# Sums of operands by accumulating DMAs, signs of weights on VectorE, and a seventh product in three parts, in a two-layer Strassen network

## The chip, the core and the metric

One core of one Trainium2 chip. The metric is device time in microseconds (us) of one execution. The engines are TensorE (PE; its weight loads are shown as PEld), VectorE (DVE), ScalarE (ACT), GpSimd (POOL) and SyncE (SP). Each works through its own list of instructions in order; semaphores make one wait for another. DMAs are issued by SP, ACT or POOL and run on 16 DMA engines.

## The reference

Attention (batch 2, 12 heads, 448 positions, head size 64) with a tanh cap on the scores, and behind it two feed-forward layers on 896 tokens of 768 numbers, with results in float32 (the weights arrive as float64):

```python
scores = cap * np.tanh(scale * np.matmul(q, k.transpose(0, 1, 3, 2)) / cap)
attn = np.exp(scores - scores.max()); attn = attn / (attn.sum() + 1e-9)
x = merge_heads(np.matmul(attn, v))                  # 896 x 768
h = x @ w_in;  g = np.maximum(h, 0) + alpha * np.minimum(h, 0);  x = g @ w_out    # layer 1, 768 -> 2048 -> 768
h = x @ w_in2; r = np.maximum(h, 0); g = r * r;                  x = g @ w_out2   # layer 2
```

## The kernel before

The tokens stand as two halves b = 0, 1 of 448 columns. A matrix product in full float32 accuracy is made of three matmuls in the faster type fp32r: each operand is split into a high part h (a copy to fp32r, on ACT) and a low part l (operand minus h, on DVE), and hh, lh and hl are added in PSUM. A "plain" product is one float32 matmul without splits. `multiply` (L193) makes either.

After the attention there are four stages. **Up, layer 1**: for each of 16 rows f of 128 features, one weight tile of 128 x 768, and for both halves a group of 6 x 3 matmuls into one PSUM bank; then L270 and L272 on ACT and L273 on DVE give the leaky ReLU g[b, f]. For f below 3 the weights (and b = 0) are made beside the attention. **Down, layer 1**: the 2048 x 768 product is done as a 2 x 2 block product in seven products P7, P1, P2, P6, P5, P4, P3 (Winograd's form), each of 4 weight tiles (`factor`) and 8 token tiles (`tokens`), for 3 PSUM banks. Their operands are sums of quarters: S3 = A11 - A21, S2 = A22 - S3, S1 = A11 + S2, S4 = A12 - S2 of the weights, T3, T2, T1, T4 of the tokens, all made in place by `sum` (L249) on DVE. P1 alone is plain (`PLAIN`, L33; L195). The results are combined on DVE (L329) and split for layer 2 (L320 on ACT, L321 on DVE). **Up and down, layer 2** are the same, with a squared ReLU (L270, and L276 in place on ACT) and the output DMA at the end (L317).

The weights come as float64 (two int32 words each), and `load` makes float32 of one tile of 128 x 768: a DMA on SP (L223) to one of two raw buffers; ACT scales the high words into w (L239); DVE shifts the low words (L240); ACT writes a half-precision product of the high word into the top half of the low word, which leaves the sign there (L233); DVE joins w and the low words (L237). There are 64 loads: 3 beside the attention, by `read` (L173), which takes the sign with an AND and an OR on DVE (L181, L183), and 61 by `load`. Of the 32 loads of each layer 16 are up tiles and 16 down quarters; the quarters come one after the other as soon as the buffers (two raw, 16 w) allow.

The order of every instruction of the four stages on PE, ACT, DVE, POOL and SP is written out by a planner in the kernel (`Plan`): it goes through the operations in a simulated time with a cost for each and a lag to its successors, and lets each engine take the ready operation with the lowest number. Operations marked `port` (on DVE and POOL) don't overlap in it.

Of the kernel before, what the change touches and what calls it, by code (L numbers as in the profile page):

```python
# [17 lines left out]
P = 128  # L18
# [34 lines left out]
class Plan:  # L53
# [4 lines left out]
    def tag(self, name, tiles):  # L58
        self.free[name], self.queue[name] = list(tiles), []

    def op(self, engine, cost, emit, reads=(), writes=(), port=False, lag=0.06):
        op = Op(len(self.ops), engine, cost, emit, port, lag)
        self.ops.append(op)
        before = []
        for buf in reads:
            before.append(buf.writer)
        for buf in writes:
            before += [buf.writer, *buf.readers]
        for other in set(before):
# [12 lines left out]
        for buf in op.bufs:  # L82
            buf.left += 1

    def order(self):
# [8 lines left out]
        while events:  # L94
# [50 lines left out]
class Net:  # L145
# [54 lines left out]
    def activate(self, g, t, ps, f):  # L200
        nc = self.nc
        nc.scalar.activation(g, ps, AF.Relu)
        nc.scalar.activation(t, ps, AF.Relu, scale=-1.0)
        nc.vector.scalar_tensor_tensor(g, t, self.slope_t[:, f:f + 1], g, op0=ALU.mult, op1=ALU.add)

    def up_now(self, f):

# [11 lines left out]
    def load(self, src):  # L219

        nc, plan, n = self.nc, self.plan, self.NC * P
        raw, w = Buf("raw"), Buf("w")
# [8 lines left out]
        def sign():
            halves = raw.tile.bitcast(F16).rearrange("p n (f t) -> p n f t", t=4)
            nc.scalar.mul(halves[:, :, :, 1], parts()[1].bitcast(F32), 2.0 ** -60)  # L233
# [11 lines left out]
    def sum(self, out, a, b, op, n, engine="DVE", inplace=True):  # L245
        nc, plan = self.nc, self.plan
        e = {"DVE": nc.vector, "POOL": nc.gpsimd}[engine]
        cost = self.dve(n) if engine == "DVE" else 0.15 + 0.0024 * n
        plan.op(engine, cost, lambda: getattr(e, op)(out.tile, a.tile, b.tile), [a, b], [out], port=True)  # L249

    def split(self, w, tags, n, engine="DVE"):
# [3 lines left out]
        e = {"DVE": nc.vector, "POOL": nc.gpsimd}[engine]  # L255
        plan.op(engine, self.dve(n) if engine == "DVE" else 0.15 + 0.0024 * n,
                lambda: e.tensor_sub(l.tile, w.tile, h.tile.bitcast(F32)), [w, h], [l], port=True)  # L257
        return h, l

    def products(self, ps, w, x, c, first, last):  # L260
        self.plan.op("PE", 3 * 0.2044 if len(w) == 2 else 0.752, lambda: self.multiply(ps.tile, [b.tile for b in w], [b.tile for b in x], c, first, last),
                     [*w, *x], [ps])

    def up(self, w, f, b, first):

        nc, S, plan, half = self.nc, self.S, self.plan, self.NF // 2
        ps, g, t = Buf("ps"), Buf("g"), Buf("t")
        for c in range(self.NC):
            self.products(ps, w, self.x[b, c], c, c == 0, c == self.NC - 1)
        plan.op("ACT", self.act(S), lambda: nc.scalar.activation(g.tile, ps.tile, AF.Relu), [ps], [g])  # L270
        if first:
            plan.op("ACT", self.act(S), lambda: nc.scalar.activation(t.tile, ps.tile, AF.Relu, scale=-1.0), [ps], [t])  # L272
            plan.op("DVE", self.dve(S), lambda: nc.vector.scalar_tensor_tensor(  # L273
                g.tile, t.tile, self.slope_t[:, f:f + 1], g.tile, op0=ALU.mult, op1=ALU.add), [t, g], [g], port=True)
        else:
            plan.op("ACT", self.act(S), lambda: nc.scalar.square(g.tile, g.tile), [g], [g])  # L276
        self.g[b, f] = g
        if b == 1 and f >= half:
            self.sum(self.g[1, f - half], g, self.g[1, f - half], "tensor_sub", S)

    def quarter(self, name, i):
        a = {"A11": 0, "S3": 1, "A12": 2, "A22": 3}[name]
        w = self.a[name, i] = self.load(self.wdown[:, a * PARTS + i])
        if name == "S3":
            self.sum(w, self.a["A11", i], w, "tensor_sub", self.NC * P)

    def factor(self, name, i, plain):

        a, n = self.a, self.NC * P
        if name == "S2":  # L290
            a[name, i] = a.pop(("S3", i))
            self.sum(a[name, i], a["A22", i], a[name, i], "tensor_sub", n)
        elif name == "S1":
            a[name, i] = a.pop(("A11", i))
            self.sum(a[name, i], a["S2", i], a[name, i], "tensor_add", n)
        elif name == "S4":
            a[name, i] = a.pop(("A12", i))
            self.sum(a[name, i], a[name, i], a["S2", i], "tensor_sub", n)
        return (a[name, i],) if plain else self.split(a[name, i], ("wh", "wl"), n)

    def tokens(self, name, k, plain):

        g, half, S = self.g, self.NF // 2, self.S
        if name == "T2":
            self.sum(g[1, k], g[0, k], g[1, k], "tensor_add", S)
        elif name == "T1":
            self.sum(g[0, k], g[1, half + k], g[1, k], "tensor_sub", S)
# [15 lines left out]
    def down(self, final):  # L323
# [4 lines left out]
        def add(t, ps, x):  # L328
            plan.op("DVE", self.dve(S), lambda: nc.vector.tensor_add(t.tile, ps.tile, x.tile), [ps, x], [t])  # L329

        def keep(t, ps):
            plan.op("ACT", self.act(S), lambda: nc.scalar.copy(t.tile, ps.tile), [ps], [t])
# [1 line left out]
        for name, a, b in (("P7", "S3", "T3"), ("P1", "A11", "B11"), ("P2", "A12", "B21"), ("P6", "S2", "T2"),  # L334
# [8 lines left out]
            for j in range(J):  # L343
# [3 lines left out]
                elif name == "P1":  # L347
                    keep(u[j], ps)
                elif name == "P6":
                    add(u[j], ps, u[j])  # L350
                    self.sum(v[j], u[j], v[j], "tensor_add", S)
                else:
                    row, col, x = {"P2": (0, 0, u), "P5": (1, 1, v), "P4": (1, 0, v), "P3": (0, 1, u)}[name]
                    if name == "P5":
                        add(u[j], ps, u[j])
                    t = ps if not final else Buf("g") if name in ("P2", "P5") else x[j]
                    add(t, ps, x[j])
                    self.put(t, row * J + j, col, final)

    def layers(self):  # L360
# [12 lines left out]
        for first, src, self.wdown in ((True, self.w1, self.w2), (False, self.w3, self.w4)):  # L373
            self.a = {}
            for f in range(self.NF):
                early = first and f < AHEAD
                w = ahead[f] if early else self.split(self.load(src[:, f]), ("wh", "wl"), self.NC * P)
# [450 lines left out]
```

## Time and profile before

| | us |
|---|---|
| median of 3 runs | 566.67 (564.88 to 567.07) |
| profiled execution, its own time | 567.58 |
| its span, first to last instruction | 565.8 |
| PE busy | 538.9 (95%) |
| PE weight loads busy | 424.9 (75%) |
| DVE busy | 405.4 (72%) |
| ACT busy | 419.6 (74%) |
| POOL busy | 2.0 (0%) |
| mean granted TensorE clock | 0.991 of full speed |

A row of a group of instructions says: line, engine, operation, output <- inputs by tile names, shapes, count | busy time in us, mean ns of one | idle time of the engine just before them and what ended it. Matmuls are pipelined: their recorded length (some 0.37 us for 448 columns) overlaps with the next, so a busy PE is not PE at its peak, and the distance from one to the next is what counts.

### The profile page before, as it was taken

To read this page: it belongs to the slowest core of one execution; us is meant where nothing else is said; L and a number is where in the kernel's file an instruction comes from. 1 tells how busy PE (TensorE), PEld (TensorE's weight loads), DVE (VectorE), ACT (ScalarE), POOL (GpSimd) and SP (SyncE) were. 2 spreads that over 40 slices of the span, in tenths; PEclk is the share of its full clock that TensorE was granted. 3 is DMA by queue.
4 is the path that set the end of the run, shared out by engine and by line. 5 is a ranking of instruction groups with operands and counts; after the bars stand their busy time and mean duration, and the time that the engine had idled before them with its cause. 6 is when DMAs were issued, how large, how long until landed. Compare 5 with 4: busy or idle time off the path is not lost.

```text
span 565.8 us, 6752 instructions
## 1 busy us (share of the span) xinstructions
PE 538.9 (95%) x2556; PEld 424.9 (75%) x2556; DVE 405.4 (72%) x574; ACT 419.6 (74%) x518; POOL 2.0 (0%) x12
## 2 busy tenths in 40 slices
PE   7889899979999997998999899999999999999996
PEld 2223345969999896758898788999999984789985
DVE  1798999465567767889999964444567579989862
ACT  6999892487889878957655479999889997354550
POOL 1000000000000000000000000000000000000000
PEclk9999999999999999999999899999999999999998
DMA  6455442053454444553000035555444553010111
GB/s 198 175 175 168 133 130 59 0 168 117 162 167 120 160 144 138 166 162 116 1 2 0 0 112 168 167 168 167 137 149 162 167 168 111 2 49 2 49 50 54
DMA packets 19576, 64.23 MB, mean 114 GB/s; under 512 B 3920, under 2 KB 10576, under 8 KB 19536
## 3 DMA queue, kind: packets, MB, share of 16 engines
q1 hardware_dynamic: 19392, 63.72, 34.8%
q8 instruction: 22, 0.36, 0.3%
q14 instruction: 18, 0.15, 0.1%
q10 hardware_dynamic: 144, 0.00, 0.0%
HBM read 60.89 MB, written 2.79 MB: 113 GB/s over the span
## 4 chain that ended last, share of the span: by engine, by line
PE 48%; ACT 28%; DVE 16%; DMA 4%; issue 2%; POOL 0%; ACTq 0%; DVEq 0%; POOLq 0%
PE ps L198 28%; ACT raw L233 14%; PE hm L198 11%; DVE w L237 3%; PE ps L195 3%; ACT wh L254 3%; PE pv L516 3%; ACT w L239 3%; DMA k<-in_kT 2%; DVE wl L257 2%; ACT g L270 2%; PE ps L466 2%; DVE raw L240 2%; DVE w L249 2%; ACT xh L254 1%
## 5 line engine op out<-in xcount | busy, mean ns | idle before, releaser
L198 PE MATMUL ps<-x,wh 128*128 128x448 f32 x576 | 166.6, 370 | 3.9 <-ACT t L272 2.7
L233 ACT ACTIVATE raw<-raw 128x768 f16<-128x768 f32 x61 | 118.5, 1943 | 22.8 <-DVE raw L240 22.8
L237 DVE SCALAR_TENSOR_TENSOR w<-w,raw 128x768 int32<-128x768 int32 x61 | 58.5, 959 | 88.1 <-ACT raw L233 88.0
L198 PEld LDWEIGHTS ps<-x,wh 128*128 128x128 f32 x576 | 108.3, 189 | 17.7 <-ACT t L272 3.6
L198 PE MATMUL ps<-x,wl 128*128 128x448 f32 x288 | 106.4, 369 | 0.4 <-DVE wl L257 0.4
L254 ACT CAST xh<-g 128x448 fp32r<-128x448 f32 x93 | 52.9, 576 | 62.9 <-PE ps L198 40.9
L198 PE MATMUL ps<-xh,wh 128*128 128x448 f32 x224 | 83.9, 374 | 6.7 <-ACT t L272 3.0
L257 DVE TENSOR_TENSOR wl<-w,wh 128x768 fp32r<-128x768 f32 x77 | 73.5, 955 | 16.4 <-ACT wh L254 15.0
L198 PE MATMUL ps<-xl,wh 128*128 128x448 f32 x224 | 82.2, 367 | 0.8 <-DVE xl L257 0.8
L198 PE MATMUL ps<-xh,wl 128*128 128x448 f32 x224 | 82.3, 367 | 0.4 <-DVE wl L257 0.4
L254 ACT CAST wh<-w 128x768 fp32r<-128x768 f32 x77 | 64.8, 842 | 6.4 <-DVE w L237 4.9
L257 DVE TENSOR_TENSOR xl<-g,xh 128x448 fp32r<-128x448 f32 x93 | 56.4, 621 | 11.5 <-ACT xh L254 10.3
L198 PEld LDWEIGHTS ps<-x,wl 128*128 128x128 f32 x288 | 54.5, 189 | 5.3 <-DVE wl L257 0.7
L239 ACT ACTIVATE w<-raw 128x768 f32<-128x768 f32 x61 | 56.1, 919 | 2.0 <-DMA raw<-in_w 2.0
L198 PE MATMUL hm<-x,wh 128*128 128x448 f32 x192 | 54.6, 366 | 0.0
L198 PEld LDWEIGHTS ps<-xh,wh 128*128 128x128 f32 x224 | 42.2, 188 | 14.9 <-ACT t L272 3.6
L198 PEld LDWEIGHTS ps<-xl,wh 128*128 128x128 f32 x224 | 42.2, 189 | 4.7 <-DVE xl L257 1.2
L198 PEld LDWEIGHTS ps<-xh,wl 128*128 128x128 f32 x224 | 42.2, 188 | 4.3 <-DVE wl L257 0.7
L481 ACT ACTIVATE E<-ps,scale_t 128x896 f32<-128x896 f32 x42 | 40.3, 1022 | 5.3 <-PE ps L466 5.3
L249 DVE TENSOR_TENSOR g<-g,g 128x448 f32<-128x448 f32 x64 | 39.0, 620 | 1.0 <-ACT g L276 0.7
L198 PEld LDWEIGHTS hm<-x,wh 128*128 128x128 f32 x192 | 36.0, 187 | 3.4
L486 ACT ACTIVATE E<-E,cap_t 128x1792 f32<-128x1792 f32 (+1 forms) x24 | 38.1, 1617 | 0.0
(96 smaller groups left out, 630.7 us busy)
## 6 DMA issues: line engine op xcount, KB each, us to landing
raw<-in_w SPq DMA_DIRECT2D x64, 768.0 KB, 4.2
out_T<-g SPq DMA_DIRECT2D x12, 224.0 KB, 2.0
k<-in_kT SPq DMA_DIRECT2D x11, 224.0 KB, 4.9
q<-in_qT SPq DMA_DIRECT2D x11, 224.0 KB, 5.1
v<-in_vT SPq DMA_DIRECT2D x6, 384.0 KB, 5.2
rb<-row SPq DMA_DIRECT2D x10, 224.0 KB, 3.7
vt<-in_vt SPq DMA_DIRECT2D x6, 64.0 KB, 5.6
r<-rows SPq DMA_DIRECT2D x20, 1.8 KB, 3.6
```

The lines of the kernel that those rows point to most:

```text
L195: self.nc.tensor.matmul(ps, w[0][:, c, :], x[0], start=first, stop=last)
L198: self.nc.tensor.matmul(ps, a[:, c, :], m, start=first and n == 0, stop=last and n == 2)
L233: nc.scalar.mul(halves[:, :, :, 1], parts()[1].bitcast(F32), 2.0 ** -60)
L237: nc.vector.scalar_tensor_tensor(bits, bits, 3, parts()[0], op0=ALU.logical_shift_left, op1=ALU.bitwise_or)
L239: plan.op("ACT", self.act(n) + 0.06, lambda: nc.scalar.mul(w.tile, parts()[1].bitcast(F32), 2.0 ** -112), [high, raw], [w])
L240: plan.op("DVE", self.dve(n, 2), lambda: nc.vector.tensor_scalar(parts()[0], parts()[0], 29, None, op0=ALU.logical_shift_right), [raw], [l ...
L249: plan.op(engine, cost, lambda: getattr(e, op)(out.tile, a.tile, b.tile), [a, b], [out], port=True)
L254: plan.op("ACT", self.act(n), lambda: nc.scalar.copy(h.tile, w.tile), [w], [h])
L257: lambda: e.tensor_sub(l.tile, w.tile, h.tile.bitcast(F32)), [w, h], [l], port=True)
L481: nc.scalar.activation(es[-1][:, n % 2], ps, AF.Tanh, scale=self.scale_t)
L486: self.nc.scalar.activation(x, x, AF.Exp, scale=self.cap_t)
L516: nc.tensor.matmul(self.pv[u][rows, g, :], self.v[u][0][:, g, c, rows], self.chunk(u, g * FULL + c)[:, e], start=c == 0, stop=False)
```

## The change

P1 becomes a product of three matmuls like the other six. In `load`, the ACT instruction for the sign goes; DVE takes the sign of the high word by an AND (with an XOR where the negated tile is wanted) and ORs it to the shifted low word. Sums S3, S2, S4 of the weights and T3, T2, T4 of the tokens are no longer made on DVE but by a DMA issued from GpSimd that adds its source to its destination. [...] S1, T1 and the sums of the results stay on DVE. In layer 2 the square moves from ACT to DVE, as -g*g or max(ps, 0)*g. The planner's costs and lags are changed. The two hooks `HALF` and `SQ` are false for every tile, so the branches that use them don't run.

```diff
-PLAIN = ("P1",)
+PLAIN = ()
+HALF = (lambda f, first: False, lambda i, a: False)
+SQ = lambda f: False
+LAND = 5.0
-    def op(self, engine, cost, emit, reads=(), writes=(), port=False, lag=0.06):
+    def op(self, engine, cost, emit, reads=(), writes=(), port=False, lag=0.15):
+                        elif op.lag > 1:
+                            end, op.lag = now + op.lag, 0.3
     def act(self, n):
-        return 0.17 + 0.00084 * n
+        return 0.05 + 0.000885 * n
     def dve(self, n, rate=1):
-        return 0.16 + 0.00103 * n if rate == 1 else 0.13 + 0.00052 * n
+        return 0.075 + 0.00103 * n if rate == 1 else 0.07 + 0.00052 * n
...
-        plan.op("DVE", self.dve(n, 2), lambda: nc.vector.tensor_scalar(parts()[0], parts()[0], 29, None, op0=ALU.logical_shift_right), [raw], [low], port=True)
-        plan.op("ACT", self.act(n) + 0.06, sign, [high, raw], [low])
+        if half:
...
+        else:
+            plan.op("DVE", self.dve(n, 2), lambda: nc.vector.tensor_scalar(parts()[1], parts()[1], -(1 << 31), None, op0=ALU.bitwise_and) if sign > 0
+                    else nc.vector.tensor_scalar(parts()[1], parts()[1], -(1 << 31), -(1 << 31), op0=ALU.bitwise_and, op1=ALU.bitwise_xor), [raw], [high], port=True)
+            plan.op("DVE", self.dve(n), lambda: nc.vector.scalar_tensor_tensor(
+                parts()[0], parts()[0], 29, parts()[1], op0=ALU.logical_shift_right, op1=ALU.bitwise_or), [raw, high], [low], port=True)
         plan.op("DVE", self.dve(n), join, [low, w, raw], [w], port=True)
...
+    def gather(self, out, a):
+        nc, plan = self.nc, self.plan
+        plan.op("POOL", 1.3, lambda: nc.gpsimd.dma_start(out.tile, a.tile, accum_op=ALU.add), [a, out], [out], lag=LAND)
...
-            plan.op("ACT", self.act(S), lambda: nc.scalar.square(g.tile, g.tile), [g], [g])
+            if minus:
+                plan.op("DVE", self.dve(S), lambda: nc.vector.scalar_tensor_tensor(
+                    g.tile, g.tile, -1.0, g.tile, op0=ALU.mult, op1=ALU.mult), [g], [g], port=True)
...
+            else:
+                plan.op("DVE", self.dve(S) + 0.06, lambda: nc.vector.scalar_tensor_tensor(
+                    g.tile, ps.tile, 0.0, g.tile, op0=ALU.max, op1=ALU.mult), [g, ps], [g])
...
-            self.sum(self.g[1, f - half], g, self.g[1, f - half], "tensor_sub", S)
+            self.gather(self.g[1, f - half], g)
...
-            self.sum(w, self.a["A11", i], w, "tensor_sub", self.NC * P)
+            self.gather(w, self.a["A11", i])
...
-            self.sum(a[name, i], a["A22", i], a[name, i], "tensor_sub", n)
+            self.gather(a[name, i], a["A22", i])
...
-            self.sum(a[name, i], a[name, i], a["S2", i], "tensor_sub", n)
+            self.gather(a[name, i], a["S2", i])
...
-            self.sum(g[1, k], g[0, k], g[1, k], "tensor_add", S)
+            self.gather(g[1, k], g[0, k])
...
-            self.sum(g[0, half + k], g[0, half + k], g[1, k], "tensor_sub", S)
+            self.gather(g[0, half + k], g[1, k])
```

The leaky ReLU takes a second tile with the negated slopes and ADD or SUBTRACT by the wanted sign; P6's and P2's additions of the results become subtractions.

## Rows read from the trace of the kernel before

**Rows 1.** Busy us (x instructions) by stage; then granted clock, DMA share, GB/s.
```profile
98.00:215.00 117.00, 113.06 (x541) 102.06 (x540) 75.08 (x107) 92.66 (x117) 0.00 (x0) 0.99 0.40 128
215.00:334.00 119.00, 112.44 (x493) 92.69 (x491) 103.12 (x157) 80.40 (x112) 0.00 (x0) 0.99 0.24 75
334.00:452.00 118.00, 117.66 (x574) 107.40 (x574) 62.66 (x87) 106.66 (x130) 0.00 (x0) 1.00 0.49 159
452.00:566.00 114.00, 106.08 (x475) 88.41 (x473) 87.93 (x133) 60.29 (x88) 0.00 (x0) 0.98 0.18 60
```

**Rows 2.** The chain that ended last: start us, length us, what.
```profile
102.28 6.76 PE hm L198 x33
...
363.71 19.63 PE ps L198 x96
```

**Rows 3.** Busy time of L195 alone in the two down stages (PE, then PEld).
```profile
215.00:334.00 119.00, 18.20 (x48) 9.11 (x48) 0.99 0.24 75
452.00:566.00 114.00, 18.31 (x48) 9.04 (x48) 0.98 0.18 60
```

**Rows 4.** The timeline's last matmul: start us, length us, what.
```profile
559.89 0.37 PE L198 MATMUL ps<-xh,wl 128*128 128x448 f32 x1
```

**Rows 5.** Waits of the weight loads from 98 us on: us, times, longest.
```profile
PEld ps L198 <- ACT t L272: 7.3, 5, 3.4
...
PEld ps L198 <- ACT wh L254: 3.1, 2, 1.8
PEld ps L198 <- ACT g L332: 2.7, 2, 1.8
PEld ps L198 <- DVE x L321: 1.8, 4, 0.4
PEld ps L198 <- DVE wl L257: 1.5, 2, 0.7
PEld ps L195 <- ACT g L332: 1.4, 2, 1.3
```

**Rows 6.** Groups of instructions, shapes kept apart.
```profile
L233 ACT ACTIVATE raw<-raw 128x768 f16<-128x768 f32 x61 | 118.5, 1943 | 22.8 <-DVE raw L240 22.8
...
L257 DVE TENSOR_TENSOR wl<-w,wh 128x768 fp32r<-128x768 f32 x77 | 73.5, 955 | 16.4 <-ACT wh L254 15.0
L254 ACT CAST wh<-w 128x768 fp32r<-128x768 f32 x77 | 64.8, 842 | 6.4 <-DVE w L237 4.9 <-PE hm L198 1.1 <-DVE w L249 0.2
L237 DVE SCALAR_TENSOR_TENSOR w<-w,raw 128x768 int32<-128x768 int32 x61 | 58.5, 959 | 88.1 <-ACT raw L233 88.0
L257 DVE TENSOR_TENSOR xl<-g,xh 128x448 fp32r<-128x448 f32 x93 | 56.4, 621 | 11.5 <-ACT xh L254 10.3
...
L254 ACT CAST xh<-g 128x448 fp32r<-128x448 f32 x93 | 52.9, 576 | 62.9 <-PE ps L198 40.9 <-PE hm L198 15.3 <-DVE g L249 5.9
...
L249 DVE TENSOR_TENSOR g<-g,g 128x448 f32<-128x448 f32 x64 | 39.0, 620 | 1.0 <-ACT g L276 0.7
...
L240 DVE TENSOR_SCALAR raw<-raw 128x768 int32<-128x768 int32 x61 | 33.9, 556 | 0.1
...
L249 DVE TENSOR_TENSOR w<-w,w 128x768 f32<-128x768 f32 x32 | 30.3, 953 | 0.1
...
L273 DVE SCALAR_TENSOR_TENSOR g<-t,slope_t,g 128x448 f32<-128x448 f32 x29 | 19.7, 680 | 7.3 <-ACT t L272 7.3
...
L183 DVE SCALAR_TENSOR_TENSOR raw<-raw 128x768 int32<-128x768 int32 x3 | 3.0, 992 | 0.1
```

**Rows 7.** DMA issues: tile, queue, count, KB each, median us to landing.
```profile
raw<-in_w SPq DMA_DIRECT2D x64, 768.0 KB, 4.2
out_T<-g SPq DMA_DIRECT2D x12, 224.0 KB, 2.0
...
vt<-in_vt SPq DMA_DIRECT2D x6, 64.0 KB, 5.6
```

**Rows 8.** DVE's timeline in the down stage of layer 1.
```profile
262.90 0.95 DVE L257 TENSOR_TENSOR wl<-w,wh 128x768 fp32r<-128x768 f32 x1
263.77 0.62 DVE L257 TENSOR_TENSOR xl<-g,xh 128x448 fp32r<-128x448 f32 x1
264.30 0.95 DVE L249 TENSOR_TENSOR w<-w,w 128x768 f32<-128x768 f32 x1
```

More of the change, by code (lines that the diff above doesn't have):

```diff
@@ L203, in activate @@
         nc.scalar.activation(t, ps, AF.Relu, scale=-1.0)
-        nc.vector.scalar_tensor_tensor(g, t, self.slope_t[:, f:f + 1], g, op0=ALU.mult, op1=ALU.add)
+        nc.vector.scalar_tensor_tensor(g, t, self.slope_t[:, f:f + 1], g, op0=ALU.mult, op1=ALU.subtract)
     def up_now(self, f):
@@ L213, in act, with load @@
     def act(self, n):
-        return 0.17 + 0.00084 * n
+        return 0.05 + 0.000885 * n
     def dve(self, n, rate=1):
-        return 0.16 + 0.00103 * n if rate == 1 else 0.13 + 0.00052 * n
-    def load(self, src):
+        return 0.075 + 0.00103 * n if rate == 1 else 0.07 + 0.00052 * n
+    def load(self, src, half, sign=1):
         nc, plan, n = self.nc, self.plan, self.NC * P
@@ L229, in parts, with underflow @@
             return self.words(raw.tile)
[L231 removed]
+        def underflow():
             halves = raw.tile.bitcast(F16).rearrange("p n (f t) -> p n f t", t=4)
[L233 removed]
+            nc.scalar.mul(halves[:, :, :, 1], parts()[1].bitcast(F32), sign * 2.0 ** -60)
         def join():
@@ L239, in load, with sum, split @@
         plan.op("ACT", self.act(n) + 0.06, lambda: nc.scalar.mul(w.tile, parts()[1].bitcast(F32), 2.0 ** -112), [high, raw], [w])
-        plan.op("DVE", self.dve(n, 2), lambda: nc.vector.tensor_scalar(parts()[0], parts()[0], 29, None, op0=ALU.logical_shift_right), [raw], [low], port=True)
-        plan.op("ACT", self.act(n) + 0.06, sign, [high, raw], [low])
+        if half:
+            plan.op("DVE", self.dve(n, 2), lambda: nc.vector.tensor_scalar(parts()[0], parts()[0], 29, None, op0=ALU.logical_shift_right), [raw], [low], port=True)
+            plan.op("ACT", 1.68, underflow, [high, raw], [low])
+        else:
[3 more added lines that the diff above has]
+                parts()[0], parts()[0], 29, parts()[1], op0=ALU.logical_shift_right, op1=ALU.bitwise_or), [raw, high], [low], port=True)
         plan.op("DVE", self.dve(n), join, [low, w, raw], [w], port=True)
         return w
-    def sum(self, out, a, b, op, n, engine="DVE", inplace=True):
+    def sum(self, out, a, b, op, n):
         nc, plan = self.nc, self.plan
[L247 to L251, printed above, removed]
+        plan.op("DVE", self.dve(n), lambda: getattr(nc.vector, op)(out.tile, a.tile, b.tile), [a, b], [out], port=True)
+    def gather(self, out, a):
+        nc, plan = self.nc, self.plan
+        plan.op("POOL", 1.3, lambda: nc.gpsimd.dma_start(out.tile, a.tile, accum_op=ALU.add), [a, out], [out], lag=LAND)
+    def split(self, w, tags, n):
         nc, plan = self.nc, self.plan
@@ L254, in split @@
         plan.op("ACT", self.act(n), lambda: nc.scalar.copy(h.tile, w.tile), [w], [h])
-        e = {"DVE": nc.vector, "POOL": nc.gpsimd}[engine]
-        plan.op(engine, self.dve(n) if engine == "DVE" else 0.15 + 0.0024 * n,
-                lambda: e.tensor_sub(l.tile, w.tile, h.tile.bitcast(F32)), [w, h], [l], port=True)
+        plan.op("DVE", self.dve(n), lambda: nc.vector.tensor_sub(l.tile, w.tile, h.tile.bitcast(F32)), [w, h], [l], port=True)
         return h, l
     def products(self, ps, w, x, c, first, last):
-        self.plan.op("PE", 3 * 0.2044 if len(w) == 2 else 0.752, lambda: self.multiply(ps.tile, [b.tile for b in w], [b.tile for b in x], c, first, last),
+        self.plan.op("PE", 3 * 0.2038 if len(w) == 2 else 0.746, lambda: self.multiply(ps.tile, [b.tile for b in w], [b.tile for b in x], c, first, last),
                      [*w, *x], [ps])
@@ L267, in up @@
         ps, g, t = Buf("ps"), Buf("g"), Buf("t")
+        minus = (b == 1) == (f >= half)
         for c in range(self.NC):
@@ L272, in up @@
             plan.op("ACT", self.act(S), lambda: nc.scalar.activation(t.tile, ps.tile, AF.Relu, scale=-1.0), [ps], [t])
+            slope = self.slope_t if minus else self.minus_t
             plan.op("DVE", self.dve(S), lambda: nc.vector.scalar_tensor_tensor(
-                g.tile, t.tile, self.slope_t[:, f:f + 1], g.tile, op0=ALU.mult, op1=ALU.add), [t, g], [g], port=True)
+                g.tile, t.tile, slope[:, f:f + 1], g.tile, op0=ALU.mult, op1=ALU.subtract if minus else ALU.add), [t, g], [g], port=True)
         else:
-            plan.op("ACT", self.act(S), lambda: nc.scalar.square(g.tile, g.tile), [g], [g])
+            if minus:
+                plan.op("DVE", self.dve(S), lambda: nc.vector.scalar_tensor_tensor(
+                    g.tile, g.tile, -1.0, g.tile, op0=ALU.mult, op1=ALU.mult), [g], [g], port=True)
+            elif SQ(f):
+                plan.op("ACT", self.act(S), lambda: nc.scalar.square(g.tile, g.tile), [g], [g])
+            else:
+                plan.op("DVE", self.dve(S) + 0.06, lambda: nc.vector.scalar_tensor_tensor(
+                    g.tile, ps.tile, 0.0, g.tile, op0=ALU.max, op1=ALU.mult), [g, ps], [g])
         self.g[b, f] = g
         if b == 1 and f >= half:
-            self.sum(self.g[1, f - half], g, self.g[1, f - half], "tensor_sub", S)
+            self.gather(self.g[1, f - half], g)
     def quarter(self, name, i):
         a = {"A11": 0, "S3": 1, "A12": 2, "A22": 3}[name]
-        w = self.a[name, i] = self.load(self.wdown[:, a * PARTS + i])
+        w = self.a[name, i] = self.load(self.wdown[:, a * PARTS + i], HALF[1](i, a), -1 if a in (0, 2) else 1)
         if name == "S3":
-            self.sum(w, self.a["A11", i], w, "tensor_sub", self.NC * P)
+            self.gather(w, self.a["A11", i])
     def factor(self, name, i, plain):
@@ L304, in tokens @@
         if name == "T2":
-            self.sum(g[1, k], g[0, k], g[1, k], "tensor_add", S)
+            self.gather(g[1, k], g[0, k])
         elif name == "T1":
-            self.sum(g[0, k], g[1, half + k], g[1, k], "tensor_sub", S)
+            self.sum(g[0, k], g[1, k], g[1, half + k], "tensor_sub", S)
         elif name == "T4":
-            self.sum(g[0, half + k], g[0, half + k], g[1, k], "tensor_sub", S)
+            self.gather(g[0, half + k], g[1, k])
         x = g[{"B11": (0, k), "T3": (1, k), "B21": (0, half + k), "T2": (1, k), "T1": (0, k), "T4": (0, half + k), "B22": (1, half + k)}[name]]
@@ L326, in down, with add @@
         u, v = ([Buf("g") for _ in range(J)] for _ in range(2))
-        def add(t, ps, x):
-            plan.op("DVE", self.dve(S), lambda: nc.vector.tensor_add(t.tile, ps.tile, x.tile), [ps, x], [t])
+        def add(t, ps, x, op="tensor_add"):
+            plan.op("DVE", self.dve(S), lambda: getattr(nc.vector, op)(t.tile, x.tile, ps.tile), [ps, x], [t])
         def keep(t, ps):
@@ L356, in down @@
                     t = ps if not final else Buf("g") if name in ("P2", "P5") else x[j]
-                    add(t, ps, x[j])
+                    add(t, ps, x[j], "tensor_sub" if name == "P2" else "tensor_add")
                     self.put(t, row * J + j, col, final)
@@ L376, in layers @@
                 early = first and f < AHEAD
-                w = ahead[f] if early else self.split(self.load(src[:, f]), ("wh", "wl"), self.NC * P)
+                w = ahead[f] if early else self.split(self.load(src[:, f], HALF[0](f, first)), ("wh", "wl"), self.NC * P)
                 for b in both:
@@ L453, in constants @@
         nc.sync.dma_start(self.slope_t, self.alpha)
-        nc.gpsimd.tensor_scalar_mul(self.slope_t, self.slope_t, -1.0)
+        self.minus_t = self.const.tile([P, self.NF], F32, name="minus_t")
+        nc.gpsimd.tensor_scalar_mul(self.minus_t, self.slope_t, -1.0)
     def product(self, u, n):
```

4 lines of the change are left out of this document (2 added, 2 removed).

## The prediction

> **What bounds the kernel now.** I read the busy time by stage first, then the groups of instructions, then what TensorE waited for. The four stages after the attention are: up projection of layer 1, its down projection, and the same of layer 2. In [rows 1] the reader is to see that TensorE (PE) is busy nearly all of each stage (113.06 of 117, 112.44 of 119, 117.66 of 118, 106.08 of 114 us), and that the second engine changes: ScalarE (ACT) is at 92.66 and 106.66 us in the two up stages, VectorE (DVE) at 103.12 and 87.93 us in the two down stages.
>
> So the floor is TensorE's. In a stretch with no wait, 96 matmuls of 448 columns take 19.63 us, 0.2045 us each; the unbroken row of second-half products starts at 102.28 [rows 2]. From there the kernel has 29 groups of 18 matmuls in layer 1, 32 in layer 2 and 2 x 6 split products of 72: 1962 matmuls, 401.2 us. The plain P1 adds 18.20 and 18.31 us [rows 3]. Without a wait PE would end at 102.3 + 437.7 = 540.0. Its last matmul ends at 559.89 + 0.37 = 560.3 [rows 4]: **20.3 us are lost**. What the weight loads waited for says where: 7.3 on L272, 3.1 on L254, 2.7 and 1.4 on L332, together 14.5 us on ACT; DVE has the smaller rows (1.8 on L321, 1.5 on L257) [rows 5]. ACT is late because each weight load keeps it for L233, 1943 ns, 118.5 us over 61 loads; L237 of DVE has 88.0 us of idle time in front of it for the same instruction [rows 6].
>
> **The change part by part.**
>
> *P1 in three products.* 48 plain matmuls (36.5 us, [rows 3]) become 144 of 0.2045 = 29.4 us: **PE -7.1 us**, on the path. It adds splits of 8 weight tiles and 16 token tiles: on ACT 8 x 0.842 + 16 x 0.576 = 15.9 us, on DVE 8 x 0.955 + 16 x 0.621 = 17.6 us [rows 6]. These lie beside PE. What is lost is a breathing space: in P1 neither engine had splits to make.
>
> *Signs on VectorE.* L233 goes 61 times: **ACT -118.5 us**. DVE keeps one one-source instruction of the form of L240 (the AND in place of the shift, 556 ns for either) and gets a scalar_tensor_tensor of strided words, which the early path already has: L183, 992 ns [rows 6]. **DVE +60.5 us.** The XOR rides in the AND, at nothing. A load's chain also loses a hop between engines: AND, OR and join run one behind the other on DVE, beside the one ACT scaling.
>
> *Sums by accumulating DMA.* Of 102 sums on L249, 48 of 448 columns (T3, T2, T4) and 24 of 768 (S3, S2, S4) leave DVE: 48 x 0.620 + 24 x 0.953 = **-52.6 us** [rows 6]. No row shows an accumulating DMA or GpSimd issuing one. From below: the 224 KB output copy lands in 2.0 us; from above: the 768 KB load takes 4.2 and the slowest form 5.6 us [rows 7]. I take 5, near the upper end, as it must read two operands. What hides it: P7's last T3 operand (k = 7) is made from the last up group, and is first used after 7/8 of P7's 72 x 0.2045 = 14.7 us, so 12.9 us after P7's start; the others have one to three whole products of lead. GpSimd's queue has nothing else in it here (POOL 0.00 in all four stages, [rows 1]), but it is in order: a gather that waits for its operand holds those behind it. Their DMAs share engines that are 0.18 to 0.49 busy, with SP's loads. If the cover were gone, each microsecond over 12.9 would cost one per layer. I cost it at 0, with 0 to 6 us for the range.
>
> The row of L240 (556 ns, where two-source instructions of the same 768 columns take some 955) shows the one-source operation running at nearly twice the rate. The Trainium skill (SBUF — State Buffer, Who interferes with whom) says of just such VectorE modes that they and GpSimd exclude one another for a whole instruction, and that GpSimd then cannot write the descriptors of its DMAs; no run here shows it yet. By that rule a gather starts later by up to one such instruction, and an AND can wait for a gather's issue. Worked out from rows: even if GpSimd held each of 72 issues for the 2.0 us of a whole short transfer [rows 7], that is 144 of 431 us, a third; a third of 61 ANDs waiting 1 us on average puts 20 us on DVE. It would change the sum by nothing as long as DVE has that room, and speaks for the second rival.
>
> *Squares.* 32 squares of layer 2 move from ACT to DVE. The nearest row is L273, 680 ns [rows 6]: **DVE +21.8 us** (bounds: 0.620 as L249, 19.8; none below). The 16 that read PSUM hold its bank until DVE has run; eight banks of 3.7 us each make that harmless unless DVE is some 10 us late.
>
> *The rest.* Costs and lags of the planner change the order on every engine. No row prices that; I put -3 to +8 us on it, and it is the main unknown. The subtract forms and the second slope tile cost nothing: same instructions, other operation; the one GpSimd multiply is off the path.
>
> **The sum.** PE's work from 102.3: 2106 matmuls x 0.2045 = 430.7, end at 533.0; the tail behind the last matmul (565.8 - 560.3 = 5.5: sums, output DMA) stays: a span of 538.5 with no wait at all. DVE in the four stages: 328.8 [rows 1] + 60.5 - 52.6 + 21.8 + 17.6 = **376 us**, against PE's 431: 87%. Records of DVE overlap when it runs without waits: L257 at 262.90 is recorded 0.95 and the next starts 0.87 later, the one at 263.77 is 0.62 and the next starts 0.53 later [rows 8]; with some 530 instructions that is up to 45 us less, so 77% to 87%. ACT goes to 340 - 118.5 + 15.9 less the squares, under 240 us, 55%: late nowhere.
>
> What becomes of the 20.3 us: the 14.5 on ACT go, as the engine has half its time free. The other 5.8 (DVE, and the lower clock behind long waits) stay. DVE becomes the second engine, at 87% or less. How much a second engine at such a share makes PE wait is shown by [rows 1]: in the third stage ACT was busy 106.66 of 118 us, 90%, and PE still 117.66 of 118; in the second DVE had 87% and PE lost 6.6. Between 0 and 7 per layer I take 1.5 each, since the third stage, like the after, has one loaded engine and one with room: +3. So 538.5 + 5.8 + 3 = a span of 547.3. The profiled execution took 567.58 for a span of 565.8, and the median of the three shown is 566.67: + 1.8 - 0.9 gives **548 us**.
>
> **Rivals.**
>
> 1. *The waits only change sides.* The ACT waits go and as many appear on DVE: the up stage of layer 2 would hold 32 loads of 556 + 992 + 959 ns, 16 splits of 955 and 32 squares of 680, 117 us of records in 32 x 18 x 0.2045 = 118 us of PE. For it: that stage. Against it: the 16 quarter loads of a layer may run into the down stage, where sums have gone. Then 20.3 us stay lost, and only the 7.1 of P1 remains: **560 us**.
>
> 2. *DVE becomes the bound and runs with holes (slower).* Place: load chains of three dependent DVE instructions in an in-order queue, with an ACT copy between join and split. PE's stretch of 458 us in the kernel before (102.3 to 560.3) is exceeded when 376 us of DVE work fill less than 82% of the time. For it: in the first stage DVE was busy only 75.08 of 117 us. Against it: those holes were waits for L233, which is gone, and the second stage got 87%. At 80% the stretch is 470 us: **579 us**. By the Trainium skill's rule above DVE's 376 would be up to 396, and the point would be 86%.
>
> 3. *Gathers land late.* At 15 to 18 us a landing, T3's last operands miss by 2 to 5 us per layer and queues behind them stall: 548 + 4 to 10, **555 us**. Against it: no DMA row is above 5.6 us [rows 7].
>
> 4. *All waits go*: 538.5 + 0.9 and a little, **540 us**. Against it: DVE's small rows lie at product boundaries, which stay.
>
> **How the numbers follow.** Forecast 0.52 (its own range 543 to 555), rival 1 0.20, rival 2 0.13, rival 3 0.08, rival 4 0.07. Half a per cent of 566.67 is 2.8 us, about what a measurement of this kernel can tell from no change. Faster than 563.8: all of the forecast, rivals 3 and 4 and most of rival 1, 0.80; within, the edges of rivals 1 and 2, 0.07; slower, rival 2, 0.13. The range is 540 to 567: it reaches over rival 1 and leaves most of rival 2 and the floor's lower edge out.
>
> **What would show it.** P1: matmuls of L198's form in place of L195, 72 per layer and product. Signs: ACT without an instruction of 1943 ns, DVE with two of about 0.96 and one of 0.56 per load. Sums: 72 DMA issues from GpSimd, landing in 4 to 6 us, none in the rows that PE waited for. DVE busy about 376 us in the four stages and ACT about 240. PE's wait rows on ACT nearly gone, and no more than some 9 us of wait in all. Wrong if DVE is above 390 us, if weight loads wait on L257 or on the join for more than 10 us, or if tokens wait for DMAs.

## The result, and the profile after

The changed kernel takes **558.53 us** (median of 4 runs, 558.18 to 562.21) against 565.77: ratio 0.9885, interval 0.9842 to 0.9928. It is faster by 7 us, where 18 were forecast; 558.53 lies in the range of 540 to 567, but the time is that of the first rival (560), not of the forecast (548). Here and below a ratio is taken over the undisturbed runs of both kernels and not from the two medians, so it differs a little from their quotient.

The profiled execution was the slowest of the four (562.21 us, span 560.4). Busy time by stage, columns as in [rows 1], at the stages' new bounds:

```profile
96.00:208.00 112.00, 112.00 (x542) 100.73 (x541) 87.43 (x116) 58.16 (x98) 12.53 (x14) 1.00 0.61 172
208.00:327.00 119.00, 109.45 (x505) 96.90 (x504) 104.97 (x160) 67.11 (x111) 19.04 (x22) 0.96 0.56 136
327.00:444.00 117.00, 116.22 (x579) 107.99 (x578) 88.38 (x123) 50.65 (x77) 12.49 (x15) 1.00 0.67 190
444.00:561.00 117.00, 106.70 (x506) 95.33 (x504) 87.53 (x131) 55.40 (x91) 19.07 (x22) 0.98 0.46 106
```

The engines' totals came out as worked out: DVE 368 us in the four stages (forecast 376), ACT 231 (under 240). The first stage is what was hoped for: TensorE is busy all of it, and the first weight load of P7 starts at 208.0, not 215.2. From there almost nothing more is gained: the down stage of layer 1 takes 119.1 us (208.0 to 327.1), where before it took 116.6 (215.2 to 331.8) *with* the plain P1. The last matmul ends at 553.7, before at 560.3 [rows 4], so the two stages of layer 2 take 226.6 us instead of 228.5, 1.9 us less, where the three-part P1 alone was to give 3.6.

Waits of the weight loads from 98 us on (answering [rows 5]; "issue" is a wait whose cause the profile doesn't show):

```profile
PEld ps L206 <- DVE xl L272: 6.5, 4, 4.2
PEld ps L206 <- issue: 4.2, 2, 3.8
PEld ps L206 <- ACT g L356: 2.4, 5, 0.9
PEld ps L206 <- ACT xh L271: 2.4, 1, 2.4
PEld ps L206 <- DVE g L353: 1.7, 3, 1.0
...
PEld ps L206 <- ACT t L288: 0.9, 4, 0.2
```

(Lines have moved: L206 is the matmul, L271 and L272 the high and low part of a split, L247 and L245 the scaling and the join of a load, L356 the copy g of a result, L288 the second ReLU, L353 and L344 the sum of a result on DVE and its copy on ACT, L266 a gather, that is an accumulating DMA.) The waits on ACT sum to 8.2 us here, where [rows 5] had 14.5 in their larger rows, and two waits of about 4 us have come. Both stand in one place, at the start of P6 of layer 1 (weight loads on the timeline):

```profile
257.56 0.19 PEld L206 LDWEIGHTS ps<-xh,wh 128*128 128x128 f32 x1 [3.78 <-issue]
...
267.11 0.28 PEld L206 LDWEIGHTS ps<-xl,wh 128*128 128x128 f32 x1 [4.23 <-DVE xl L272]
```

and they lower the clock behind them (the mean granted clock of the next window, third column from the end, is 0.78; a part of it ran at 1.2 instead of 2.4 GHz):

```profile
240.00:260.00 20.00, 16.55 (x78) 14.61 (x76) 17.92 (x27) 10.76 (x19) 10.55 (x13) 0.96 1.06 249
260.00:280.00 20.00, 16.15 (x64) 14.21 (x63) 13.47 (x20) 8.87 (x15) 1.72 (x2) 0.78 0.69 151
```

142 matmuls fit in these 40 us, where some 197 would at 0.203 us: some 11 us are lost here.

The first of the two has no cause at the weight load ("issue"), but the profile names one for the matmul that belongs to it, and VectorE's timeline shows why that came late:

```profile
253.20 0.56 DVE L252 TENSOR_SCALAR raw<-raw 128x768 int32<-128x768 int32 x1 [1.21 <-ACT w L247]
...
256.82 0.62 DVE L353 TENSOR_TENSOR ps<-g,ps 128x448 f32<-128x448 f32 x1
...
257.59 0.44 PE L206 MATMUL ps<-xh,wh 128*128 128x448 f32 x1 [3.43 <-DVE ps L353]
```

L353 sums the first result of P2, whose last matmul ended at 254.2. In VectorE's list it stands behind the AND (L252), OR and join (255.95, below) of the last load of layer 1, and that load's data landed only at 252.24.

For the second wait the chain leads back through the sums of S2:

```profile
239.85 5.60 DMA raw<-in_w
...
250.88 13.70 DMA w<-w
...
265.12 0.86 POOL w L266
```

A raw load, and then a gather in a burst of them, 13.7 us from issue to landing (the last row is a gather that waited for it). ACT stands in its list before the high part of S2, with the last copy of P2's results behind it. VectorE waits for that copy, and the low part that TensorE needs (266.44) comes next in VectorE's list:

```profile
252.26 0.91 ACT L247 ACTIVATE w<-raw 128x768 f32<-128x768 f32 x1 [2.97 <-DMA raw<-in_w]
...
264.61 0.83 ACT L271 CAST wh<-w 128x768 fp32r<-128x768 f32 x1 [4.58 <-DMA w<-w]
...
265.90 0.62 DVE L345 TENSOR_TENSOR x<-ps,x 128x448 fp32r<-128x448 f32 x1 [4.36 <-ACT x L344]
```

The DMA issues, the accumulating ones in the last two rows (the first answers to [rows 7]):

```profile
raw<-in_w SPq DMA_DIRECT2D x64, 768.0 KB, 4.6
g<-g POOLq DMA_DIRECT2D x45, 224.0 KB, 6.3
w<-w POOLq DMA_DIRECT2D x24, 384.0 KB, 7.2
```

**Why S2 is so late** is seen in what it adds, A22, which is loaded last. When the join of the last loads starts on DVE, after:

```profile
238.87 0.95 DVE L245 SCALAR_TENSOR_TENSOR w<-w,raw 128x768 int32<-128x768 int32 x1
243.56 0.94 DVE L245 SCALAR_TENSOR_TENSOR w<-w,raw 128x768 int32<-128x768 int32 x1
249.64 0.94 DVE L245 SCALAR_TENSOR_TENSOR w<-w,raw 128x768 int32<-128x768 int32 x1
255.95 0.95 DVE L245 SCALAR_TENSOR_TENSOR w<-w,raw 128x768 int32<-128x768 int32 x1
```

and before:

```profile
255.22 0.96 DVE L237 SCALAR_TENSOR_TENSOR w<-w,raw 128x768 int32<-128x768 int32 x1 [0.66 <-ACT raw L233]
260.95 0.96 DVE L237 SCALAR_TENSOR_TENSOR w<-w,raw 128x768 int32<-128x768 int32 x1
```

The 29 loads of layer 1 end at 257 instead of 262, though ACT has lost 1.94 us on each. They never sped up: from the first join to the last it is one in 5.3 us either way (5.31 before, 5.26 after). What ACT waits for has changed. Before, and then after:

```profile
ACT w L239 <- DMA raw<-in_w: 2.0, 4, 0.9
```

```profile
ACT w L247 <- DMA raw<-in_w: 43.4, 25, 4.9
ACT wh L271 <- DMA w<-w: 10.1, 4, 4.6
ACT xh L271 <- DMA g<-g: 9.1, 4, 4.2
```

There are two raw buffers. Each goes through a DMA (4.6 us), the scaling (0.91), AND, OR and join on DVE (0.56 + 0.96 + 0.95, with other work between) before the next load may start. The AND waits for the scaling, as it overwrites the word that it reads. The next load goes out as soon as a join has ended, before:

```profile
240.36 0.96 DVE L237 SCALAR_TENSOR_TENSOR w<-w,raw 128x768 int32<-128x768 int32 x1 [0.69 <-ACT raw L233]
...
241.34 0.33 SPq L223 DMA_DIRECT2D raw<-in_w  x1
```

and after (the join at 238.87 above):

```profile
239.85 0.33 SPq L231 DMA_DIRECT2D raw<-in_w  x1
```

In both kernels this gap is 0.03 us behind each of the last 26 joins of layer 1, so two buffers and their round trip set the pace in both. The round trip's mean over these 26 loads is 10.65 us before and 10.55 after. From the scaling's end to the join it takes 2.79 us before (the sign on ACT) and 2.63 after (AND and OR on DVE); the scaling starts 0.83 us sooner after the landing; the DMA takes 5.15 us instead of 4.24, beside the gathers (4.01 with all sums on VectorE, below). The freed ACT now waits for this round trip.

### The profile page after: what moved, and what is told of

Its sections match the earlier page's. It is cut to its first block, busy times and chain, and to the rows that moved or that the text cites. A ratio compares the mean times of both kernels' runs of the same rounds, so it can differ in the third digit from the quotient of the medians.

```text
span 560.4 us, 7124 instructions
## 1 busy us (share of the span) xinstructions
PE 533.4 (95%) x2604; PEld 435.2 (78%) x2604; DVE 444.9 (79%) x619; ACT 310.7 (55%) x449; POOL 65.1 (12%) x84
## 3 DMA queue, kind: packets, MB, share of 16 engines
HBM read 60.89 MB, written 2.79 MB: 114 GB/s over the span
## 4 chain that ended last, share of the span: by engine, by line
PE 48%; issue 26%; DMA 13%; DVE 7%; ACT 4%; POOL 1%; POOLq 0%; ACTq 0%; DVEq 0%
PE ps L206 31%; PE hm L206 8%; DMA raw<-in_w 5%; DMA g<-g 4%; PE pv L541 3%; PE ps L491 3%; DMA w<-w 2%; ACT E L506 1%; ACT E L511 1%; DVE w L245 1%; DVE raw L254 1%; DMA k<-in_kT 1%; ACT w L247 1%; DVE xl L272 1%; DVE s L527 1%
## 5 line engine op out<-in xcount | busy, mean ns | idle before, releaser
L206 PE MATMUL ps<-x,wh 128*128 128x448 f32 x576 | 164.6, 367 | 0.8 <-ACT g L286 0.8
L206 PEld LDWEIGHTS ps<-x,wh 128*128 128x128 f32 x576 | 107.4, 187 | 12.7 <-ACT g L286 1.1
L206 PE MATMUL ps<-x,wl 128*128 128x448 f32 x288 | 105.1, 365 | 0.0
L206 PE MATMUL ps<-xh,wh 128*128 128x448 f32 x256 | 96.9, 378 | 7.4 <-DVE ps L353 3.4
L206 PE MATMUL ps<-xl,wh 128*128 128x448 f32 x256 | 96.2, 376 | 5.1 <-DVE xl L272 5.1
L271 ACT CAST xh<-g 128x448 fp32r<-128x448 f32 x106 | 59.6, 568 | 67.7 <-PE ps L206 39.4
L206 PE MATMUL ps<-xh,wl 128*128 128x448 f32 x256 | 95.5, 373 | 0.0
L272 DVE TENSOR_TENSOR wl<-w,wh 128x768 fp32r<-128x768 f32 x85 | 80.9, 952 | 17.0 <-ACT wh L271 15.6
L271 ACT CAST wh<-w 128x768 fp32r<-128x768 f32 x85 | 71.1, 836 | 37.8 <-PE ps L206 15.9
L266 POOL DMA_DIRECT2D g<-g x45 | 40.1, 924 | 371.1 <-DVE g L290 172.2
L247 ACT ACTIVATE w<-raw 128x768 f32<-128x768 f32 x61 | 55.6, 911 | 43.7 <-DMA raw<-in_w 43.4
L272 DVE TENSOR_TENSOR xl<-g,xh 128x448 fp32r<-128x448 f32 x106 | 64.6, 618 | 17.6 <-ACT xh L271 16.9
L206 PEld LDWEIGHTS ps<-xh,wh 128*128 128x128 f32 x256 | 49.2, 192 | 16.7 <-issue 4.2
L254 DVE SCALAR_TENSOR_TENSOR raw<-raw 128x768 int32<-128x768 int32 x61 | 58.3, 956 | 1.1
L245 DVE SCALAR_TENSOR_TENSOR w<-w,raw 128x768 int32<-128x768 int32 x61 | 58.2, 954 | 0.9
L206 PEld LDWEIGHTS ps<-x,wl 128*128 128x128 f32 x288 | 54.0, 187 | 4.9 <-DVE wl L272 0.4
L206 PEld LDWEIGHTS ps<-xl,wh 128*128 128x128 f32 x256 | 49.3, 193 | 10.7 <-DVE xl L272 6.5
L206 PE MATMUL hm<-x,wh 128*128 128x448 f32 x192 | 54.5, 365 | 0.0
L206 PEld LDWEIGHTS ps<-xh,wl 128*128 128x128 f32 x256 | 49.4, 193 | 4.5
L286 ACT ACTIVATE g<-ps 128x448 f32<-128x448 f32 x45 | 24.3, 541 | 38.0 <-PE ps L206 38.0
L206 PEld LDWEIGHTS hm<-x,wh 128*128 128x128 f32 x192 | 36.0, 187 | 3.0
```

Of the source, the lines that this page charges most:

```text
L206: self.nc.tensor.matmul(ps, a[:, c, :], m, start=first and n == 0, stop=last and n == 2)
L254: plan.op("DVE", self.dve(n), lambda: nc.vector.scalar_tensor_tensor(parts()[0], parts()[0], 29, parts()[1], op0=ALU.logical_shift_right, ...
L266: plan.op("POOL", 1.3, lambda: nc.gpsimd.dma_start(out.tile, a.tile, accum_op=ALU.add), [a, out], [out], lag=LAND)
L272: plan.op("DVE", self.dve(n), lambda: nc.vector.tensor_sub(l.tile, w.tile, h.tile.bitcast(F32)), [w, h], [l], port=True)
```

## The experiments

Three theories. **A**: the gathers land late, and what is behind them in the lists waits. **B**: VectorE is too full, which is the second rival in a mild form. **C**: the loads are paced by the two raw buffers, so that S2 can't be had in time, whoever adds it. Ratios are to the kernel before, with the 95% interval.

**The changed kernel again.** 

> The changed kernel unaltered, for a second profile. Theory A (gathers land late): the waits of the weight loads stand again in front of P6 of layer 1 (some 4 + 4 us, followed by matmuls at the lower clock) and P7 of layer 2 (2.4 us), and the accumulating DMAs issued just before take 8 to 14 us to land. Theory B (VectorE is too full): the waits move about from execution to execution, and stand behind splits on L272 that no DMA held up. Either way 558 us.


Measured 560.69 us, 0.9925 (0.9904 to 0.9947). In a second profile P6 waits again, 3.73 and 4.50 us, with a lower clock after it, and the first of the two again for L353 (254.61) behind the last load's join (253.74). In place of the 2.35 us in P7 of layer 2 there are 3.17 us in the up stage before it. The place at P6 is a property of the kernel, so A or C.

**All sums on VectorE.**
```diff
-        plan.op("POOL", 1.3, lambda: nc.gpsimd.dma_start(out.tile, a.tile, accum_op=ALU.add), ...)
+        plan.op("DVE", self.dve(...), lambda: nc.vector.tensor_add(out.tile, a.tile, out.tile), ...)
```


> The changed kernel with all 72 sums back on VectorE (additions in place of the accumulating DMAs), nothing else undone. Theory A: the waits in front of P6 and P7 go, 52.6 us of work come back to VectorE and find room: 550 to 556 us. Theory B: VectorE goes from 445 to 497 us busy and TensorE waits for it more: 568 us or above.


Measured 564.90 us, 0.9991 (0.9969 to 1.0013). (The changed kernel keeps A11, A12 and some token tiles negated, so these sums are additions here too.) Between the two: the DMAs are worth 4 us here. The waits at P6 shrink to 2.81 and 0.68, but others come, 9.65 in front of P5 of layer 2 and 4.59 in the down stage of layer 1. Neither A nor B alone.

**S2 alone on VectorE.**
```diff
-            self.gather(a[name, i], a["A22", i])
+            self.sum(a[name, i], a[name, i], a["A22", i], "tensor_add", n)
```


> The changed kernel with the four sums S2 of each layer on VectorE (8 of 72), the other 64 still by DMA. Theory A: the wait in front of P6 (8 us and the low clock after it) goes: 550 to 553 us. Theory B: no change, 557 to 560. Theory C (the loads of A22 themselves come late): a part of the wait stays, 555.


Measured 554.38 us, 0.9801 (0.9762 to 0.9839). Eight sums moved back bring 6 us. Of the two waits at P6 the second, behind the S2 gather, is gone. Of the first 2.83 us are left: L353 starts at 254.43, right behind the last load's join (253.56). So the landing of these eight was one half of the matter, and the late loads, C, the other.

**P1 plain again** (`PLAIN = ("P1",)`). 

> The changed kernel with P1 as a plain product again: TensorE +7.1 us, 15.9 us less on ScalarE and 17.6 less on VectorE, and 3.5 us more for A22 and S2 before P6. Theory A: P6's wait shrinks by 3.5, so 562 us. Theory B: VectorE's room is worth more than 7.1: 556 or below.


Measured 561.84 us, 0.9941 (0.9912 to 0.9970): 1 us more than the changed kernel beside it, for 7.1 us more of TensorE. The time is A's. By the two profiles, though, the down stage of layer 1 takes 3.2 us longer with P1 plain (120.7 against 117.4), nearly all that P1 adds there, and it is the stages of layer 2 that take 2.5 us less (226.0 against 228.5); why was not taken apart. VectorE's relief of 17.6 us doesn't bring it to 556 or below: against B.

**A longer landing in the planner** (`LAND = 14.0`). 

> The changed kernel with the planner told that an accumulating DMA takes 14 us and not 5; only the order of the lists changes. Theory A1 (the order is the fault: copies on ScalarE stand in its list ahead of other work and wait for DMAs that the planner thought landed): 552 to 556 us, the waits on ScalarE for DMAs shrink. Theory A2 (the sums S2 can't be had earlier, since their operand A22 is loaded last): as the changed kernel, 559 to 561 us.


Measured 562.21 us, 0.9940 (0.9915 to 0.9966): nothing gained. The waits of about 4 us at P6 are gone, but one of 5.46 us on a high part ends some 18 us into the down stage instead, and P6 starts at 261.1 where it started at 257.6. This order is no better; that no order would be is not shown.

**A22 loaded before A12.**
```diff
-            for name in ("A12", "A22"):
+            for name in ("A22", "A12"):
```


> The changed kernel with the four quarters A22 of each layer loaded before the four A12. Theory A2 (S2 waits for the loads of A22): S2 can be issued some 20 us earlier, P6's wait goes, and A12 is late for P2 at most by a little: 551 to 556 us. Theory A1 (only the order behind DMAs counts): 557 to 561 us.


Measured 559.47 us, 0.9875 (0.9834 to 0.9916): not the gain that A2 gave; the number is A1's. But the wait moves to P2, which now waits for A12's parts (1.93, 0.78, 2.87, 1.64), and the loads of layer 1 end no sooner (last join at 259.76). Whatever is loaded last is late. That is C.

**A third raw buffer, and S2 on VectorE.**
```diff
-SLOTS = {"raw": 2, ... "xl": 4}
+SLOTS = {"raw": 3, ... "xl": 3}
-            plan.tag("raw", [self.raw[:, (AHEAD + n) % 2] for n in range(2)])
+            plan.tag("raw", [self.raw[:, (AHEAD + n) % 2] for n in range(2)] + [lp.tile([P, self.NC, P], I64, name="raw2")])
```


> The changed kernel with S2 on VectorE and a third raw buffer (one low-part token buffer fewer makes room). Theory C (the pace of the loads, some 5.2 us each with two raw buffers, is what is late at P6): all A22 are there before P6 and it beats S2 on VectorE alone (554.4): 545 to 551 us. If the pace of VectorE sets the loads, no change: 553 to 556 us.


Measured **543.12 us, 0.9599 (0.9560 to 0.9637)**. The last quarters of layer 1 are joined 29 us before P6 starts (252.8):

```profile
214.87 0.94 DVE L245 SCALAR_TENSOR_TENSOR w<-w,raw 128x768 int32<-128x768 int32 x1
218.48 0.95 DVE L245 SCALAR_TENSOR_TENSOR w<-w,raw 128x768 int32<-128x768 int32 x1
222.63 0.95 DVE L245 SCALAR_TENSOR_TENSOR w<-w,raw 128x768 int32<-128x768 int32 x1
```

No clock is lost any more, and the down stage of layer 1 takes 109 us:

```profile
206.00:315.00 109.00, 105.36 (x507) 94.04 (x506) 106.03 (x162) 68.54 (x112) 16.21 (x19) 1.00 0.50 129
315.00:430.00 115.00, 115.00 (x577) 107.87 (x576) 97.67 (x133) 51.43 (x78) 12.35 (x14) 1.00 0.66 193
```

VectorE is busy for 106.03 of 109 us there, and TensorE still for 105.36. B is out.

**The third raw buffer alone.** 

> The changed kernel with a third raw buffer (one low-part token buffer fewer makes room), all 72 sums by DMA. Theory C (two raw buffers pace the loads at 5.2 us, so the gathers of S2 start late): most of the gain of 543 us comes without S2 on VectorE: 543 to 548 us. Theory A (the gathers land late whatever the loads do): 552 us or above.


Measured 546.04 us, 0.9641 (0.9602 to 0.9679). With the loads in time the S2 gathers do little harm: with these sums on VectorE it was 543.12, and the intervals of the two ratios overlap. A load of layer 1 is joined every 4.17 us, the round trip of 12.5 us through three buffers. ACT's wait for raw data, 43.4 us after, is here

```profile
ACT w L247 <- DMA raw<-in_w: 6.2, 5, 3.7
```

**The third raw buffer, all sums on VectorE.** 

> The changed kernel with a third raw buffer and all 72 sums on VectorE. If the DMAs' 52.6 us of relief matter when the loads are in time: 552 to 560 us. If VectorE has the room: 545 us.


Measured 546.69 us, 0.9674 (0.9639 to 0.9710), with VectorE 484.9 of 544.3 us busy (89%). So where the loads are in time the 72 DMAs are worth nothing that can be measured.

**One token buffer fewer, two raw buffers** (the control, as the third raw buffer took its room). 

> The changed kernel with one low-part token buffer fewer and still two raw buffers: the control of the third raw buffer. Theory C (the raw buffer gave the gain): 558 to 562 us. Rival (the other order of the lists gave it): 550 us or below.


Measured 561.10 us, 0.9925 (0.9898 to 0.9953): no gain. The raw buffer gave it. Beside this control the third buffer brings the down stage of layer 1 from 119.1 to 109.5 us and the two stages of layer 2 from 227.4 to 220.7: the slow loads cost in layer 2 as well. A third buffer also changes the order that the planner writes; that share was not taken apart.

Now the parts on the kernel before.

**The signs alone** (AND and OR on VectorE as in the change's diff). 

> The kernel before with the signs on VectorE alone (AND and OR there, the 1.94 us of ScalarE gone; sums, P1, squares and the planner's costs as before). Theory A: the first up stage gains its 6 us, the rest little: 558 to 562 us. Theory B (VectorE too full, 466 us busy): waits come back in the down stages: 566 us or above.


Measured 566.74 us, 1.0010 (0.9985 to 1.0035): 118 us less on ScalarE are worth nothing alone. That is B's number, but the loads of layer 1 end at 265, no sooner than before, and with a third raw buffer (below) the same VectorE work takes 8 us less. The waits have moved, and the largest comes from the loads, with no gather about: it ends at 267.37 and is for the second weight tile of P6, whose S2 is summed at 265.51. Its A22 was joined at 252.41, but in VectorE's list the sum stands behind the join of the last load (264.11).

```profile
PEld ps L198 <- ACT wh L255: 6.0, 1, 6.0
...
PEld ps L198 <- DVE wl L258: 5.0, 3, 3.1
PEld ps L198 <- DVE xl L258: 4.5, 2, 4.0
```

**The third raw buffer on the kernel before.** 

> The kernel before with a third raw buffer (and one low-part token buffer fewer). Theory C in full (before, ScalarE's 3.7 us a load and its other work held the loads at nearly the same pace, so a third buffer can do little there): 560 to 567 us. Rival (the buffers alone were the bound before too): 550 us or below.


Measured 575.88 us, 1.0202 (1.0175 to 1.0229): slower, which no theory had. The loads do run ahead, the last ends at 239. TensorE waits longer for L270 (0.7 before), for L320 (3.7 us, before 0.9) and for VectorE's low parts xl (4.2, before 1.2), not for L272 (7.3 before). A landed load now waits 4.7 us for ScalarE (1.7 before); that the early loads' long instructions there push back its copies is argued, not shown by itself:

```profile
PEld ps L198 <- ACT g L270: 7.4, 3, 3.7
PEld ps L198 <- ACT t L272: 7.2, 4, 2.9
```

**One token buffer fewer on the kernel before.** 

> The kernel before with one low-part token buffer fewer and still two raw buffers. If the fewer token buffers made the kernel before slow with a third raw buffer: 573 us or above. If the third raw buffer did (loads that run ahead put more of ScalarE's long instructions in front of its evacuations): 564 to 568 us.


Measured 562.87 us, 0.9947 (0.9918 to 0.9975): a little below both, so the slowdown just seen came from the raw buffer.

**Signs and third raw buffer on the kernel before.** 

> The kernel before with the signs on VectorE and the third raw buffer (P1 plain, sums on VectorE, squares on ScalarE, costs as before). Theory C (ScalarE's sign and the two raw buffers bounded the loads together, so that only taking both away helps): 550 to 557 us, loads of layer 1 done by 230. Rival (the sums or P1 are needed too): 563 us or above.


Measured 558.04 us, 0.9865 (0.9837 to 0.9892), loads done by 232. One us outside what C gave, but the sense is plain: the one alone gains nothing, the other alone loses 10 us, both together gain 8.

**P1 in three products alone.** 

> The kernel before with P1 in three products and nothing else. If the 7.1 us of TensorE come through: 559 us. If the splits it adds to two engines that are already late eat them: 563 to 568 us.


Measured 581.70 us, 1.0284 (1.0255 to 1.0313): 7.1 us less of TensorE, and 16 us slower, 13 more than the worse forecast. The splits meet engines that are late: the waits on VectorE's low parts (xl 1.2 before, wl 1.5) and on ScalarE's copies of results (L332, 2.7 and 1.4 before) grow. Those on L272 (7.3 before) and on the high part wh (1.7, before 3.1) don't.

```profile
PEld ps L198 <- ACT t L272: 7.1, 4, 3.5
PEld ps L198 <- DVE xl L257: 7.0, 5, 4.0
PEld ps L198 <- ACT g L332: 6.8, 4, 4.9
PEld ps L198 <- DVE wl L257: 4.9, 2, 4.1
```

## Why the prediction was wrong

*The floor and the totals held.* DVE's 376 (368 measured) and ACT's 240 us (231) were right. So was PE's work: with the third raw buffer layer 2 takes 220.7 us, and 1080 matmuls of 0.2045 are 220.9. VectorE at 87% was rightly held to be nearly harmless: with the loads in time and all sums on it, it is busy for 409 of the 443 us of the four stages (92%), and the kernel runs in 546.7. The best variant's 543.12 is 4 us above the floor that was worked out.

*The step that failed: "the 14.5 on ACT go, as the engine has half its time free".* It counted engines only. The loads are a loop of DMA, ScalarE and VectorE through two raw buffers, whose round trip was 10.65 us before and 10.55 after: a load in 5.3 us both times. Before, ScalarE had other work to do meanwhile and waited only 2.0 us for raw data, so no row of waits named the buffers; with its part taken away it waits 43.4 us, at the same pace. The sentence on the load's chain was wrong too: AND, OR and join don't run "beside the one ACT scaling" but behind it, and the lost hop brought 0.16 us. The first stage did gain its 7 us, as the waits of its weight loads went (5.9 us before, 1.0 after). The quarters of the down stage came only 5 us sooner, and what was gained in front of them was waited away at P6. The late loads cost there twice: their A22 goes into S2, and their instructions stand in VectorE's list ahead of the sum of P2's result. With a third raw buffer the changed kernel takes 546.0, the forecast's time.

*"The others have one to three whole products of lead" was wrong for S2.* The lead was counted from the product that uses S3. But S2 also needs A22, whose joins at 255.22 and 260.95 stood in the trace of before, while by the forecast's own pitch P6 starts at 102.3 + 106.7 + 3 x 14.7 = 253. By the same pitch its third and fourth weight tiles are wanted at 260 and 264, so the lead was 4 and 2 us, less than the landing of 5 that was taken, and every microsecond of landing counted. S2 on VectorE gave 6 us.

*Landing: 5 us taken, 6.3 and 7.2 measured, 13.7 in the burst at S2.* (The longest of all took 15.1.) The forecast went by DMA shares of 0.18 to 0.49 before; the sums raised them to 0.46 to 0.67, and to 1.06 where T2 and S2 go out together beside loads.

*The residue (+3 for VectorE) and rival 1.* Rival 1 had the time (560) by waits that move to VectorE. The largest row of waits after is on a low part, but VectorE was only the last link: without the buffer's limit its 89% cost nothing that can be measured. That the measured time is rival 1's is luck. Rival 3 had a part of the mechanism (gathers late, lists blocked behind) but put it at T3 and for all landings of 15 us; one burst at S2 was enough. At T3 it cost something in layer 2 alone: P7's last token tile (k = 7) waits 2.35 us there, for a gather that took 8.1 us. The cover of 12.9 us was counted from P7's start (442.3), but this gather went out only at 450.5. Rival 2 fell.

*The exclusion of VectorE and GpSimd* (the Trainium skill, SBUF — State Buffer, Who interferes with whom) showed no price on VectorE: the AND takes 555 ns in the median beside 72 gathers and 557 with none (all sums on VectorE). A gather's own issue takes 0.86 us in the median, 1.6 at most; 14 of the 72 take over 0.9, 5 of these beside an AND, so whether the exclusion lengthened them is not shown.

*What stays open.* Why that S2 gather took 13.7 us was not taken apart: DMAs queued before them, the loads beside them, or GpSimd's order. Nor was it tried which of the squares, the planner's costs and P1 gives the 11 us between signs with a third buffer (558.0) and the same with the rest of the change but for the DMAs (546.7).

## What to carry to other kernels

Before costing the relief of an engine, write down the loops that run through buffers: the round trip divided by the number of buffers is a bound beside the engines (here 10.6 / 2 and 12.5 / 3 us). The rows of waits don't name it as long as every engine in the loop has other work meanwhile; look instead whether each load goes out the moment a buffer comes free. For an operand, take the lead from the last of its inputs to arrive in the trace, the loaded one too, not from the step that uses the other. Gains of edits don't add: here the signs, the third buffer and P1, each alone on the kernel before, gained nothing or lost up to 16 us, and the whole change with the third buffer gave 19 to 23.

## What the runs showed of the hardware

In this kernel the accumulating DMAs inside SBUF keep the DMA engines busy for longer per byte than the loads do. Queues of the changed kernel (packets, MB, share of 16 engines over the span):

```profile
q1 hardware_dynamic: 19392, 63.72, 35.5%
q0 software_dynamic: 10368, 20.45, 20.0%
```

0.98% of the span per MB against 0.56%: 1.75 times as much. The record counts each added byte once, though both operands have to be read for it. Per packet the two are nearly alike (0.173 and 0.164 us of one DMA engine), and the accumulating DMAs' packets are smaller, 1.97 against 3.29 KB on average; whether the adding or the size of the packets makes the difference was not tried.
